# Two transposes of gathered rows ahead of expert weight loads, later counts, and loop registers read behind the last scatter

## The chip, the cores and the metric

The kernel runs on one core of one Trainium2 chip. The metric is the device time of the program in microseconds (us). TensorE (PE) multiplies, VectorE (DVE) and ScalarE (ACT) do elementwise work, GpSimd (POOL) does some of it and issues the indirect DMAs, and SyncE (SP) issues most other DMAs: weight loads, and the DMAs that transpose.

## The reference

Eight batches of eight heads of attention over 576 rows of 64 values, in which only scores within tau of the row's maximum count. Its result, 4608 rows of 512, goes through a mixture of eight experts, one expert to a row:

```python
scores = scale * np.matmul(q, k.transpose(0, 1, 3, 2))
thresh = np.max(scores, axis=-1, keepdims=True) - tau
scores = np.where(scores >= thresh, scores, -1000000000.0)
attn = softmax(scores); out = np.matmul(attn, v)      # x: rows of all heads
expert_idx = np.argmax(x @ w_gate, axis=1)            # gate_w: its softmax value
for e in range(8):
    xe = x[expert_idx == e]
    h = np.maximum(xe @ w1[e], 0.0)                   # 512 -> 1024
    out[expert_idx == e] = gate_w * (h @ w2[e])       # 1024 -> 512
```

## The kernel before, in words

The program has two parts that overlap. The first is the attention of 32 pairs of heads. After each batch its 576 rows of x are routed: gate logits (`lg`), rank of each row within its expert (`rk`), and a scatter of the rows into a DRAM buffer `xs`, sorted by expert (L714, issued by POOL). The second part works through slots of 128 rows of `xs`. For a slot `m`, POOL gathers the rows (L956), SP issues a DMA that transposes them (L962, into `xTm_m`; for slots 3 and 4 it writes into the tail of the tile `R_0`, and the profile calls it `R<-R`), PE multiplies with w1 (`h_m`), ACT and DVE apply the ReLU and split the result in two half-precision parts (`hl_m`), PE multiplies with w2 (`y_m`), ACT scales (`o_m`, L1054) and POOL scatters the rows into the result (L1057).

Weights come in pieces of 128 x 1024 floats. `wf_e_c_w` is chunk `c` of w1 (`w` = 0) or w2 (`w` = 1) of expert `e`; SP loads it (`load_w`, L905) into one of eight buffers. ACT and DVE split it into halves (L918, L919): `wb1_0`, `wb2_0` for even experts, `wb1_1`, `wb2_1` for odd ones. A load into a buffer waits until the piece before it in that buffer has been split.

The first slots are filled before attention has ended: slots 0 to 2 (`NF` = 3) from counts after an early batch, slots 3 and 4 from counts (`pc_1`, function `tables1`) later, and the slots from 5 on once the last batch's counts are there. These last counts (`tables2`) need the ranks of batch 7 and a small matmul `pc_2` on PE. `tables3` (`table_late`) works out the late slots' row lists, the experts whose weights a late slot needs (`esi`) and the bounds `from` and `total` of a loop for rows that no slot holds. That loop (`For_i`, L1339) comes last in the program, and here runs no time. Its two bounds are loaded into a register of each engine at L1337 and L1338.

What sets the order. Up to step `KEND - 16` of the attention each engine's order is written out by hand; after that a scheduler places each instruction on its engine from a timeline of its own, in which the program's order, data dependencies and priorities count. The program's order comes from tables of due times (`plan`, `after(n, f)`: `f` goes n steps on; `phase(7, n)`: step n of the last batch; `w1a`, `w1b`: offsets at which weight pieces go). An engine runs its list in order; an instruction that waits holds all that stands behind it.

Of the kernel before, what the change touches and what calls it, by code (L numbers as in the profile page):

```python
# [44 lines left out]
CAP = NTOK  # L45

TUNE = dict(
    lead=10, cast=1, sl=10, ll=15, sp0=6, sps=0, lv=-9, sv=-2, av=2, tr=4, d=2, lg=5, d5=2, d6=2, d7=1, lg7=9, km=16, rate=15, dh=1, do=3, w1d=5, plv=1, xv=3, so=0, sto=0, ord=0, sc=5, fa=3, fd=4, wa1=-70, wa2=-86, wl1=-28, wl2=-6, avb=2, route=1, ranks=7, pp=8, ew=4, maskat=0, w1a=-40, w1b=3,
)


# [1 line left out]
def kernel(  # L53
# [594 lines left out]
    def route(b, n, dist, Lj, w, got):  # L648
# [38 lines left out]
        def ranks():  # L687
# [32 lines left out]
                sent.add((b, j))  # L720

            if b in TABLES:
                after(phase(7, 10 if b == B - 3 else 18), TABLES[b], FRONT)
            for j in range(n):
                after(6 + dist * j, lambda j=j: send(j))

# [164 lines left out]
    def open_pool(i):  # L891
# [5 lines left out]
        wb1.append(mp.tile([P, 4, 2 * F], F16, name=f"wb1_{i}", bufs=1))  # L897
        wb2.append(mp.tile([P, 4, 2 * F], F16, name=f"wb2_{i}", bufs=1))

    def load_w(e, w, c):  # L900

        i = int(e != 0)
        wq[e, w, c] = wf = pools[i].tile([P, F], F32, tag="wf", name=f"wf_{e}_{c}_{w}", bufs=2 + 6 * i)
        if e in range(E):
            nc.sync.dma_start(wf, w12[e, :, c, w])  # L905
            return
        if e not in regs:
            regs[e] = nc.sync.value_load(T["esi"][0:1, e - E:e - E + 1], min_val=0, max_val=E - 1)
        nc.sync.dma_start(wf, w12[ds(regs[e], 1), :, c, w].rearrange("o p f -> (o p) f"))
# [17 lines left out]
    def fetch(m):  # L927
# [21 lines left out]
        for z in range(1 + (late(m) and tail(m) > 0)):  # L949
            dst = xT[:, i]  # L950
            if late(m):
                Rm = row(B - 1, z if m == "x" else (2 * m + z) % 5)
                w = P + tail(m)
                dst = xT.rearrange("p i c t -> p (i c t)")[:, 0:8 * w].rearrange("p (c t) -> p c t", c=8)
                d["xT"], dst = dst, dst[:, :, P * z:P + tail(m) * z]
            dma = nc.gpsimd.indirect_dma_start(  # L956
                Rm, None, xs[:, :], bass.IndirectOffsetOnAxis(ap=idx[:, z:z + 1].bitcast(U32), axis=0)
            )
            for x in sends:
                tc.add_manual_dep(dma.ins, x.name, SYNC)  # L960
            tc.add_to_no_dep_group("xs", dma.ins)
            nc.sync.dma_start_transpose(dst, Rm[0:tail(m) if z else P, 0:DM].bitcast(F16))  # L962
            gt = small.tile([P, 2], I32, tag="gt", name=f"gt_{m}_{z}", bufs=6)
            gw, ti = gt.bitcast(F32)[:, 0:1], gt[:, 1:2]

            def where(Rm=Rm, gw=gw, ti=ti, z=z):
                nc.vector.tensor_copy(gw, Rm.bitcast(F32)[:, DM:DM + 1])
                to = Rm[:, DM + 1:DM + 2]
                if z:
                    nc.gpsimd.tensor_tensor(ti, to, to, ALU.add)  # L970
                    if tail(m) < P2:
                        nc.gpsimd.tensor_tensor(ti, ti, ti, ALU.add)
                    to = ti
                nc.gpsimd.tensor_tensor(ti, to, bad[:, z:z + 1], ALU.add)

            if m == "x":
                where()
            else:
                after(6, where)
            d["gw"].append(gw)  # L980
            d["ti"].append(ti)
# [11 lines left out]
    def gemm1(g):  # L993
# [14 lines left out]
        for u in range(8 // per):  # L1008
            ph = ps_sc.tile([P, 512], F32, tag="sc", name=f"h_{g[0]}_{u}")
            k = 0  # L1010
            for q in range(per):
                f = slice((per * u + q) * P, (per * u + q + 1) * P)
                o = ph[:, q * w:(q + 1) * w]
                for c in range(4):
                    for z, (wh, xh) in enumerate(((0, 0), (0, 1), (1, 0))):
                        x = xT[:, 2 * c + xh] if late(g[0]) else xT[:, 0:n, 2 * c + xh]
                        tie = g == groups[0] and u == q == c == z == 0
                        emit(o, Wt[:, c, wh, f], x, tie=tie, start=c == 0 and z == 0, stop=c == 3 and z == 2)
                        k += w
                        if k >= 12 * P and (q, c, z) != (per - 1, 3, 2):  # L1020
                            k -= 12 * P
                            yield
            moe(chunk[0] + DH, lambda: True, lambda ph=ph, u=u: relu(ph, u))
            yield

    def gemm2(g):
        d = ms[g]
# [2 lines left out]
        for i in range(len(d["ti"])):  # L1030
# [17 lines left out]
            def leave(i=i, m=m, y=y, half=half, r=r):  # L1048
# [7 lines left out]
                def put():  # L1056
                    dma = nc.gpsimd.indirect_dma_start(  # L1057
                        to, bass.IndirectOffsetOnAxis(ap=d["ti"][i].bitcast(U32), axis=0), o, None,
                        bounds_check=top - 1, oob_is_err=False,
                    )  # L1060
                    if m != "x":
                        tc.declare_no_dep(dma.ins, group="out", reason="each row of the result is written once")
                        tc.add_to_no_dep_group("out", dma.ins)
# [97 lines left out]
    def tables2():  # L1161
# [4 lines left out]
        nc.vector.tensor_scalar(s_e, s_e, float(NE * P), None, ALU.add)  # L1166
        nc.vector.tensor_tensor(s_e, s_e, cnt, ALU.min)
        T[2] = cnt, s_e
        after(20, tables3)

    def tables3():
        T["row"], T["bad"], T["esi"], T["from"], T["total"], static = table_late(*T[2])
# [2 lines left out]

    def experts():

        for i in range(len(groups) + 1):
            if i < len(groups):
                assert there(groups[i], 0)  # L1180
                yield from gemm1(groups[i])
                past[0] = groups[i][-1]
            if i:
                assert there(groups[i - 1], 1)
                yield from gemm2(groups[i - 1])
                past[1] = groups[i - 1][-1]

    def room():
        ldp.close()
# [144 lines left out]
            chunk[0] += 1  # L1334


    total = nc.values_load(T["total"][0:1, 0:1], min_val=0, max_val=NLX)  # L1337
    start = nc.values_load(T["from"][0:1, 0:1], min_val=0, max_val=NL)  # L1338
    with tc.For_i(start, total) as m:  # L1339
        idx = small.tile([P, 2], I32, tag="idx", name="idx_x", bufs=1)  # L1340
        nc.vector.tensor_copy(idx.unsqueeze(1), T["row"][:, ds(m, 1)])
# [67 lines left out]
```

## Time and profile before

| what | value |
|---|---|
| median of 3 runs | 952.98 us (950.48 to 954.14) |
| the profiled execution's own time | 956.04 us |
| its span, first to last instruction | 953.9 us |
| mean granted TensorE clock | 0.986 |
| PE busy | 910.9 us, 95% of the span |
| DVE, ACT, POOL busy | 643.5, 618.3, 560.9 us |
| bytes moved by DMA | 158.14 MB, mean 166 GB/s |

The profiled execution lasts 2.1 us longer than its span and 3.1 us longer than the median of the runs. Busy time of an engine does not count the issuing of DMAs, so SP has none; its work is seen in the rows `SPq`, which are its queue of instructions. "idle before <-releaser" on a row of a timeline says how long the engine stood idle ahead of it and what let it go on. The columns of the table of windows are the stretch, its length, then busy time and count for each engine, then the granted clock, the mean busy share of the DMA engines and the bytes that they moved in GB/s.

### The profile page before, as it was taken

Reading aid. Unit: us, or ns where it says so; the run is one execution under the profiler, and the core shown is the slowest. Engines: PE = TensorE matmul, PEld = TensorE weight load, DVE = VectorE, ACT = ScalarE, POOL = GpSimd, SP = SyncE. Lnnn points to the kernel's source line nnn. Section 1 sums busy time; section 2 is a strip of 40 time slices with the busy share of each in tenths; the row PEclk is TensorE's granted clock in tenths of the full one; section 3 lists DMA queues with packets and bytes.
Section 4 is the critical chain, followed back from the end, with each engine's and each line's share of the span. In section 5 each row is a group of like instructions: output and inputs, shape, how many; then the busy total and the mean of one; then the engine's idle time right before and its main releaser. Section 6 shows DMA issues by size and latency. Waiting matters only on the chain. (4 is left out here: it accounts for less than half of the span.)

```text
span 953.9 us, 25125 instructions
## 1 busy us (share of the span) xinstructions
PE 910.9 (95%) x9983; PEld 641.9 (67%) x9983; DVE 643.5 (67%) x1322; ACT 618.3 (65%) x1042; POOL 560.9 (59%) x482
## 2 busy tenths in 40 slices
PE   4899999999999999999998997999999999999995
PEld 1377777676777777776765966776667766667773
DVE  7989898989898889897986767535143333514561
ACT  4788988888989988888877744335243342524551
POOL 7678787998989989989867625431212121221121
PEclk8899999999999999999999998999999999999998
DMA  7554464585674956756737798986474656547630
GB/s 196 134 139 113 120 150 127 147 184 124 170 162 131 182 128 165 167 134 153 137 95 152 207 283 261 291 228 196 135 243 120 211 156 185 168 142 235 215 121 25
DMA packets 179859, 158.14 MB, mean 166 GB/s; under 512 B 136153, under 2 KB 152027, under 8 KB 179740
## 3 DMA queue, kind: packets, MB, share of 16 engines
q1 hardware_dynamic: 127158, 99.94, 42.1%
q10 hardware_dynamic: 43590, 27.39, 10.9%
q0 software_dynamic: 8992, 29.18, 9.4%
q8 instruction: 80, 1.31, 0.6%
q14 instruction: 39, 0.32, 0.1%
HBM read 90.56 MB, written 19.17 MB: 115 GB/s over the span
## 5 line engine op out<-in xcount | busy, mean ns | idle before, releaser
L489 POOL TENSOR_TENSOR pl<-e,ph 128x1024 f16<-128x1024 f32 x95 | 204.6, 2156 | 52.1 <-ACT ph L488 48.3
L415 DVE TENSOR_REDUCE nm<-s 128x1 f32<-128x512 f32 (+1 forms) x320 | 201.3, 634 | 5.6 <-PE st L388 1.0
L388 PEld LDWEIGHTS <-wb 128*128 128x128 f16 x2304 | 186.4, 99 | 25.9 <-issue 7.7
L388 PE MATMUL y<-wb,hl 128*128 128x512 f16 (+2 forms) x1104 | 196.3, 347 | 0.0
L388 PE MATMUL h<-xTm,wb 128*128 128x256 f16 (+3 forms) x2112 | 191.5, 251 | 2.7 <-issue 2.6
L919 DVE SCALAR_TENSOR_TENSOR wb<-wf,wb 128x1024 f16<-128x1024 f32 x96 | 115.5, 1236 | 58.1 <-ACT wb L918 56.3
L388 PEld LDWEIGHTS <-hl 128*128 128x128 f16 (+2 forms) x1104 | 89.1, 98 | 97.5 <-issue 1.3
L483 DVE SCALAR_TENSOR_TENSOR e<-st,e 128x512 f32<-128x512 f32 x192 | 129.0, 674 | 37.4 <-POOL pl L489 23.2
L403 PE MATMUL s<-QK 128*128 128x512 f16 (+3 forms) x640 | 139.1, 294 | 12.4 <-POOL QK L135 8.1
L480 ACT ACTIVATE e<-st,ntau 128x512 f32<-128x512 f32 x192 | 130.0, 688 | 23.9 <-PE st L388 22.7
L405 PE MATMUL s<-ck,CQ 128*128 128x512 f16 (+3 forms) x640 | 143.5, 292 | 0.5 <-DMA ck<-lo 0.5
L452 PE MATMUL st<-QK 128*128 128x512 f16 (+3 forms) x640 | 137.1, 291 | 5.0 <-DVE e L465 2.6
L388 PE MATMUL st<-CQ,ck 128*128 128x512 f16 (+3 forms) x640 | 132.1, 288 | 0.8 <-DMA CQ<-ptT 0.7
L1057 POOL DMA_INDIRECT out_dram<-o,gt x39 | 41.9, 1074 | 139.0 <-ACT o L1054 128.0
L1005 ACT ACTIVATE hl<-h 128x512 f16<-128x512 f32 (+2 forms) x78 | 44.6, 572 | 115.2 <-PE h L388 96.2
L918 ACT ACTIVATE wb<-wf 128x1024 f16<-128x1024 f32 x96 | 97.6, 1049 | 31.0 <-DMA wf<-in_w_dram 14.0
L531 PE MATMUL av<-vf,e 128*128 128x65 f32 (+1 forms) x1024 | 116.4, 251 | 0.0
L464 ACT ACTIVATE e<-st,ntau_f 128x512 f32<-128x512 f32 (+1 forms) x160 | 94.4, 611 | 26.2 <-PE st L388 23.3
L531 PEld LDWEIGHTS av<-vf,e 128*128 128x128 f32 (+1 forms) x1024 | 101.5, 165 | 0.2
L488 ACT CAST ph<-e 128x1024 f16<-128x1024 f32 x96 | 99.4, 1036 | 1.1 <-DVE e L483 0.9
L535 PE MATMUL av<-vop,pl 128*128 128x65 f16 x768 | 96.5, 193 | 0.0
L534 PE MATMUL av<-vop,ph 128*128 128x64 f16 x768 | 96.2, 193 | 0.0
(225 smaller groups left out, 1482.2 us busy)
## 6 DMA issues: line engine op xcount, KB each, us to landing
wf<-in_w_dram SPq DMA_DIRECT2D x96, 512.0 KB
qkf<-in_qk_dram ACTq DMA_DIRECT2D x29, 576.0 KB
vf<-in_v_dram ACTq DMA_DIRECT2D x30, 320.0 KB
QK<-hi SPq DMA_DIRECT2D x61, 144.0 KB
QK<-hi SPq DMA_DIRECT2D x61, 72.0 KB
QK<-lo SPq DMA_DIRECT2D x61, 72.0 KB
ck<-lo SPq DMA_DIRECT2D x61, 72.0 KB
CQ<-hi SPq DMA_DIRECT2D x61, 64.0 KB
```

Of the source, the lines that this page charges most:

```text
L388: x = nc.tensor.matmul(*a, **kw).ins
L403: nc.tensor.matmul(sc[rows, oc], d["QA"][a][:, cols], d["KB"][a][:, CH[c]], start=True, stop=False)
L405: nc.tensor.matmul(sc[rows, oc], d["CQ"][:, at:at + cols.stop - cols.start], d["CK"][a][:, CH[c]], start=False, stop=True,)
L415: nc.vector.tensor_reduce(o, sc[:, 0:width(t)], axis=AX.X, op=ALU.max, negate=True)
L452: nc.tensor.matmul(sc[rows, oc], d["KB"][a][:, cols], d["QA"][a][:, CH[c]], start=True, stop=False)
L480: nc.scalar.activation(pf, sc, AF.Exp, bias=ntau, scale=0.125 / SS)
L483: nc.vector.scalar_tensor_tensor(pf, sc, 0.0, pf, ALU.is_ge, ALU.mult)
L488: nc.scalar.copy(h, pd)
L489: (nc.vector if (n, t) in PLV else nc.gpsimd).tensor_tensor(l, pd, h, ALU.subtract)
L531: nc.tensor.matmul(av[rows, a], d["Pf"][t][:, q], vf[:, tv], start=False, stop=last)
L918: nc.scalar.activation(o[:, :, 0], x, AF.Copy, scale=SW)
L919: nc.vector.scalar_tensor_tensor(o[:, :, 1], x, SW, o[:, :, 0], ALU.mult, ALU.subtract)
```

## The change

Five things are changed. (1) The two transposes of slots 3 and 4 are remembered (`turned`), and each weight load of experts 1 and 2 that is written after them gets an order edge behind the second of them. The edge is for the scheduler alone; no semaphore comes of it. (2) The pieces of w1 go by `w1a` = -34 where it was -40, and the last batch's tables at step 22 of the batch where it was 18. (3) `tables3` comes 150 steps after the last counts where it was 20. (4) The order of the two multiplications around slot 3 is turned: `gemm2` of slot 2 is written ahead of `gemm1` of slot 3, and the first matmul of slot 3 is tied to that place. (5) POOL copies the loop's two bounds into a tile `ends` behind the last scatter, and the registers of all engines are loaded from `ends`.

```diff
--- before.py
+++ after.py
@@ -45,7 +45,7 @@
 CAP = NTOK
 
 TUNE = dict(
-    lead=10, cast=1, sl=10, ll=15, sp0=6, sps=0, lv=-9, sv=-2, av=2, tr=4, d=2, lg=5, d5=2, d6=2, d7=1, lg7=9, km=16, rate=15, dh=1, do=3, w1d=5, plv=1, xv=3, so=0, sto=0, ord=0, sc=5, fa=3, fd=4, wa1=-70, wa2=-86, wl1=-28, wl2=-6, avb=2, route=1, ranks=7, pp=8, ew=4, maskat=0, w1a=-40, w1b=3,
+    lead=10, cast=1, sl=10, ll=15, sp0=6, sps=0, lv=-9, sv=-2, av=2, tr=4, d=2, lg=5, d5=2, d6=2, d7=1, lg7=9, km=16, rate=15, dh=1, do=3, w1d=5, plv=1, xv=3, so=0, sto=0, ord=0, sc=5, fa=3, fd=4, wa1=-70, wa2=-86, wl1=-28, wl2=-6, avb=2, route=1, ranks=7, pp=8, ew=4, maskat=0, w1a=-34, w1b=3,
 )
 
 
@@ -720,7 +720,7 @@
                 sent.add((b, j))
 
             if b in TABLES:
-                after(phase(7, 10 if b == B - 3 else 18), TABLES[b], FRONT)
+                after(phase(7, 10 if b == B - 3 else 18 if b < B - 1 else 22), TABLES[b], FRONT)
             for j in range(n):
                 after(6 + dist * j, lambda j=j: send(j))
 
@@ -897,12 +897,17 @@
         wb1.append(mp.tile([P, 4, 2 * F], F16, name=f"wb1_{i}", bufs=1))
         wb2.append(mp.tile([P, 4, 2 * F], F16, name=f"wb2_{i}", bufs=1))
 
+    turned = {}
+    BEHIND = mybir.DependencyInfo(mybir.DependencyClass.NoSync, mybir.DependencyReason.SCHED_ONLY)
+
     def load_w(e, w, c):
 
         i = int(e != 0)
         wq[e, w, c] = wf = pools[i].tile([P, F], F32, tag="wf", name=f"wf_{e}_{c}_{w}", bufs=2 + 6 * i)
         if e in range(E):
-            nc.sync.dma_start(wf, w12[e, :, c, w])
+            dma = nc.sync.dma_start(wf, w12[e, :, c, w])
+            if e in (1, 2) and NF + 1 in turned:
+                tc.add_manual_dep(dma.ins, turned[NF + 1].ins.name, BEHIND)
             return
         if e not in regs:
             regs[e] = nc.sync.value_load(T["esi"][0:1, e - E:e - E + 1], min_val=0, max_val=E - 1)
@@ -959,7 +964,7 @@
             for x in sends:
                 tc.add_manual_dep(dma.ins, x.name, SYNC)
             tc.add_to_no_dep_group("xs", dma.ins)
-            nc.sync.dma_start_transpose(dst, Rm[0:tail(m) if z else P, 0:DM].bitcast(F16))
+            turned[m] = nc.sync.dma_start_transpose(dst, Rm[0:tail(m) if z else P, 0:DM].bitcast(F16))
             gt = small.tile([P, 2], I32, tag="gt", name=f"gt_{m}_{z}", bufs=6)
             gw, ti = gt.bitcast(F32)[:, 0:1], gt[:, 1:2]
 
@@ -1014,7 +1019,7 @@
                 for c in range(4):
                     for z, (wh, xh) in enumerate(((0, 0), (0, 1), (1, 0))):
                         x = xT[:, 2 * c + xh] if late(g[0]) else xT[:, 0:n, 2 * c + xh]
-                        tie = g == groups[0] and u == q == c == z == 0
+                        tie = g in (groups[0], groups[NF]) and u == q == c == z == 0
                         emit(o, Wt[:, c, wh, f], x, tie=tie, start=c == 0 and z == 0, stop=c == 3 and z == 2)
                         k += w
                         if k >= 12 * P and (q, c, z) != (per - 1, 3, 2):
@@ -1022,6 +1027,8 @@
                             yield
             moe(chunk[0] + DH, lambda: True, lambda ph=ph, u=u: relu(ph, u))
             yield
+
+    put_last = [None]
 
     def gemm2(g):
         d = ms[g]
@@ -1058,6 +1065,7 @@
                         to, bass.IndirectOffsetOnAxis(ap=d["ti"][i].bitcast(U32), axis=0), o, None,
                         bounds_check=top - 1, oob_is_err=False,
                     )
+                    put_last[0] = dma.ins
                     if m != "x":
                         tc.declare_no_dep(dma.ins, group="out", reason="each row of the result is written once")
                         tc.add_to_no_dep_group("out", dma.ins)
@@ -1166,7 +1174,7 @@
         nc.vector.tensor_scalar(s_e, s_e, float(NE * P), None, ALU.add)
         nc.vector.tensor_tensor(s_e, s_e, cnt, ALU.min)
         T[2] = cnt, s_e
-        after(20, tables3)
+        after(150, tables3)
 
     def tables3():
         T["row"], T["bad"], T["esi"], T["from"], T["total"], static = table_late(*T[2])
@@ -1175,15 +1183,13 @@
 
     def experts():
 
-        for i in range(len(groups) + 1):
-            if i < len(groups):
-                assert there(groups[i], 0)
-                yield from gemm1(groups[i])
-                past[0] = groups[i][-1]
-            if i:
-                assert there(groups[i - 1], 1)
-                yield from gemm2(groups[i - 1])
-                past[1] = groups[i - 1][-1]
+        for i, w in [
+            (i - w, w) for i in range(len(groups) + 1) for w in ((1, 0) if i == NF else (0, 1))
+            if 0 <= i - w < len(groups)
+        ]:
+            assert there(groups[i], w)
+            yield from (gemm1, gemm2)[w](groups[i])
+            past[w] = groups[i][-1]
 
     def room():
         ldp.close()
@@ -1334,8 +1340,11 @@
             chunk[0] += 1
 
 
-    total = nc.values_load(T["total"][0:1, 0:1], min_val=0, max_val=NLX)
-    start = nc.values_load(T["from"][0:1, 0:1], min_val=0, max_val=NL)
+    ends = tp.tile([P, 2], I32, name="ends")
+    for i, x in enumerate(("total", "from")):
+        tc.add_manual_dep(nc.gpsimd.tensor_copy(ends[:, i:i + 1], T[x]).ins, put_last[0].name, BEHIND)
+    total = nc.values_load(ends[0:1, 0:1], min_val=0, max_val=NLX)
+    start = nc.values_load(ends[0:1, 1:2], min_val=0, max_val=NL)
     with tc.For_i(start, total) as m:
         idx = small.tile([P, 2], I32, tag="idx", name="idx_x", bufs=1)
         nc.vector.tensor_copy(idx.unsqueeze(1), T["row"][:, ds(m, 1)])
```

Three places show what moves. The first is on SP and PE around the routing of batch 7. SP before, from the ninth last instruction ahead of the `R_0` transposes (`xTg_7` are the transposes of batch 7's rows for its gate logits, and stand above these rows):

```order
L905 DMA wf_2_1_0_10871<-in_w12_dram 128x1024
L905 DMA wf_1_3_0_10898<-in_w12_dram 128x1024
L905 DMA wf_2_0_1_10942<-in_w12_dram 128x1024
L905 DMA wf_1_0_1_10974<-in_w12_dram 128x1024
L905 DMA wf_2_2_0_10978<-in_w12_dram 128x1024
L905 DMA wf_2_1_1_11003<-in_w12_dram 128x1024
L905 DMA wf_1_1_1_11016<-in_w12_dram 128x1024
L905 DMA wf_2_3_0_11023<-in_w12_dram 128x1024
L905 DMA wf_1_2_1_11073<-in_w12_dram 128x1024
L962 DMA_TRANSPOSE R_0_197<-R_0_197 128x8x128 x2
L905 DMA wf_2_2_1_11078<-in_w12_dram 128x1024
L905 DMA wf_1_3_1_11151<-in_w12_dram 128x1024
```

SP now, from the `xTg_7` transposes on:

```order
L616 DMA_TRANSPOSE xTg_7_0_10690<-R_1_198 128x8x128 x2
L616 DMA_TRANSPOSE xTg_7_2_10720<-R_1_198 128x8x128 x2
L616 DMA_TRANSPOSE xTg_7_4_10732<-Rh_1_200 128x8x128
L967 DMA_TRANSPOSE R_0_197<-R_0_197 128x8x128 x2
L908 DMA wf_1_3_0_10890<-in_w12_dram 128x1024
L908 DMA wf_2_0_0_10934<-in_w12_dram 128x1024
L908 DMA wf_1_0_1_10966<-in_w12_dram 128x1024
L908 DMA wf_2_1_0_10970<-in_w12_dram 128x1024
L908 DMA wf_2_0_1_10995<-in_w12_dram 128x1024
L908 DMA wf_1_1_1_11008<-in_w12_dram 128x1024
L908 DMA wf_2_2_0_11015<-in_w12_dram 128x1024
```

The two transposes stood behind nine weight loads and now stand ahead of them, right behind the gate's; `wf_2_0_0`, which stood ahead of the gate's transposes, follows too. On PE, the last counts stood before the first matmul of slot 3, with the ranks and a last piece of slot 2 ahead:

```order
L696 MATMUL rk_7_10987<-was_7_10893,ones_151 128x40
L388 LDWEIGHTS hl_2_0_10901
L388 MATMUL y_2_0_11159<-wb2_0_9263,hl_2_0_10901 128x512
L388 LDWEIGHTS ones_151
L388 MATMUL pc_2_11179<-run_173,ones_151 128x8
L388 LDWEIGHTS wb1_0_9262
L388 MATMUL h_3_0_11030<-R_0_197,wb1_0_9262 128x128
```

Now slot 2's `y` ends and slot 3 begins with no counts between them:

```order
L388 MATMUL y_2_0_11022<-wb2_0_9263,hl_2_0_10893 128x512
L388 LDWEIGHTS hl_2_0_10893
L388 MATMUL y_2_0_11022<-wb2_0_9263,hl_2_0_10893 128x512
L388 LDWEIGHTS wb1_0_9262
L388 MATMUL h_3_0_11079<-R_0_197,wb1_0_9262 128x128
```

The counts' matmul `pc_2` now stands in the first half of slot 4's `h_4`. Further on PE now runs `y_3`, `y_4`, `h_5`, `h_6`, `y_5`, `h_7`, `y_6`, `h_8`; before it ran `y_3` with the first part of `h_5` inside, the rest of `h_5`, `y_4`, `h_6`, `y_5`, `h_7`, `y_6`, `h_8`. The number of PE's instructions is the same.

The second place is SP around the transposes of the late slots. Before:

```order
L905 DMA wf_2_2_1_11078<-in_w12_dram 128x1024
L905 DMA wf_1_3_1_11151<-in_w12_dram 128x1024
L1337 TENSOR_LOAD total_11460
L1337 ISA x2
L962 DMA_TRANSPOSE xTm_5_11044<-R_1_198 128x8x128
L905 DMA wf_2_3_1_11155<-in_w12_dram 128x1024
L905 DMA wf_3_0_0_11242<-in_w12_dram 128x1024
L962 DMA_TRANSPOSE xTm_6_11163<-R_1_198 128x8x128
L905 DMA wf_3_1_0_11335<-in_w12_dram 128x1024
L962 DMA_TRANSPOSE xTm_7_11329<-R_1_198 128x8x128
L905 DMA wf_3_0_1_11464<-in_w12_dram 128x1024
L905 DMA wf_3_2_0_11468<-in_w12_dram 128x1024
```

Now:

```order
L908 DMA wf_2_2_1_11075<-in_w12_dram 128x1024
L908 DMA wf_2_3_1_11122<-in_w12_dram 128x1024
L908 DMA wf_3_0_0_11245<-in_w12_dram 128x1024
L908 DMA wf_3_1_0_11335<-in_w12_dram 128x1024
L908 DMA wf_3_0_1_11377<-in_w12_dram 128x1024
L908 DMA wf_3_2_0_11381<-in_w12_dram 128x1024
L908 DMA wf_3_1_1_11440<-in_w12_dram 128x1024
L908 DMA wf_3_3_0_11468<-in_w12_dram 128x1024
L967 DMA_TRANSPOSE xTm_5_11027<-R_1_198 128x8x128
L908 DMA wf_3_2_1_11499<-in_w12_dram 128x1024
L908 DMA wf_3_3_1_11558<-in_w12_dram 128x1024
L967 DMA_TRANSPOSE xTm_6_11092<-R_1_198 128x8x128
```

`xTm_5`, which had eleven weight loads between the gate's transposes and itself, now has nineteen, and all but the last two pieces of expert 3 stand ahead of it. The loads of `total` into SP's register are gone from here; the four of `esi` stand behind `xTm_6`.

The third place is the end of POOL's list, behind the scatters of the last slots. Before:

```order
L1057 DMA out_0_dram<-o_34_1_15205,gt_34_1_14264 18432x128
L1057 DMA out_0_dram<-o_35_0_15235,gt_35_0_14485 4608x512
L1337 TENSOR_LOAD total_11460
L1338 TENSOR_LOAD from_11458
L1339 COMPARE_AND_BRANCH
```

Now:

```order
L1064 DMA out_0_dram<-o_34_1_15205,gt_34_1_14264 18432x128
L1064 DMA out_0_dram<-o_35_0_15235,gt_35_0_14485 4608x512
L1345 COPY ends_15240<-total_12440 128x1
L1345 COPY ends_15240<-from_12438 128x1
L1346 TENSOR_LOAD ends_15240
L1347 TENSOR_LOAD ends_15240
L1348 COMPARE_AND_BRANCH
```

The two register loads have two copies ahead of them on POOL. On PE, ACT, DVE and SP, the loads of `total` and `from`, which stood at several places, now read `ends`, and so follow the copies.

## The prediction

> **What bounds the kernel now.** I first read the page's table of the span in 40 slices and its busy times.
>
> ```profile
> span 953.9 us, 25125 instructions
> PE 910.9 (95%) x9983; PEld 641.9 (67%) x9983; DVE 643.5 (67%) x1322; ACT 618.3 (65%) x1042; POOL 560.9 (59%) x482
> PE   4899999999999999999998997999999999999995
> PEclk8899999999999999999999998999999999999998
> ```
>
> PE is busy for 95% of the span, and its instructions stay the same in number and kind. So the time can change only where PE stands idle or runs at a lowered clock. The slices show one such dip inside, at the 25th (572 to 596 us), and the ends. The timeline of PE around the dip tells what it waits for.
>
> ```profile
> 567.04 8.79 PE L388 MATMUL y<-wb,hl 128*128 128x512 f16 x40
> 575.83 0.38 PE L388 MATMUL y<-wb,hl 128*128 128x512 f16 x1
> 579.09 0.19 PE L388 MATMUL pc<-run,ones 128*128 128x8 f16 x1 [2.88 <-DVE posi L706]
> 580.02 6.90 PE L388 MATMUL h<-R,wb 128*128 128x128 f16 x73 [0.74 <-DMA R<-R]
> 606.88 5.34 PE L388 MATMUL y<-wb,hl 128*128 128x512 f16 x24
> 612.06 5.52 PE L388 MATMUL h<-xTm,wb 128*128 128x128 f16 x96
> 635.06 10.64 PE L388 MATMUL h<-xTm,wb 128*128 128x256 f16 x96
> ```
>
> PE first waits 2.88 us for the ranks of batch 7 (through the last counts' matmul, `pc`), and then 0.74 us for slot 3's transpose. An `h` of a 128-row slot costs 5.52 us and a `y` 5.34. At 635.06 the first wide slot, `h_8`, begins; I take it as the point up to which before and after are compared. The windows view, cut at the ends of these stretches, gives the clock and what the DMA engines carried.
>
> ```profile
> 560.00:576.20 16.20, 16.20 (x179) 10.33 (x175) 7.60 (x25) 4.91 (x8) 4.50 (x6) 1.00 1.04 350
> 576.20:580.02 3.82, 0.19 (x2) 0.13 (x2) 3.02 (x14) 1.92 (x5) 1.38 (x2) 0.84 1.13 276
> 580.02:585.64 5.62, 5.62 (x54) 5.62 (x54) 5.31 (x26) 0.18 (x1) 4.40 (x5) 0.50 0.91 290
> 585.64:596.34 10.70, 8.74 (x142) 7.82 (x141) 7.18 (x18) 6.41 (x8) 6.00 (x6) 1.00 0.77 206
> 606.88:635.06 28.18, 26.95 (x267) 17.84 (x265) 8.28 (x32) 8.14 (x11) 8.30 (x10) 1.00 0.95 258
> ```
>
> PE is idle for 3.82 - 0.19 = 3.63 us, and in the 5.62 us that follow the granted clock is 0.50, half of full speed: 2.81 us more. Of the rest, 10.70 - 8.74 = 1.96 and 28.18 - 26.95 = 1.23 us are short stops that the timeline puts down to "issue". Now SP's queue, to see why the transpose was late.
>
> ```profile
> 561.11 12.82 SPq L905 DMA_DIRECT2D wf<-in_w_dram  x9
> 574.11 4.63 SPq L962 DMA_TRANSPOSE R<-R  x2
> 590.73 2.59 SPq L962 DMA_TRANSPOSE xTm<-R  x1
> 564.03 0.99 POOL L956 DMA_INDIRECT R<-xs,row  x1 [2.64 <-DVE row L749]
> 565.33 0.97 POOL L956 DMA_INDIRECT R<-xs,row  x1 [0.30 <-issue]
> ```
>
> The rows of slots 3 and 4 were asked for at 564.03 and 565.33, but their transposes are issued only at 574.11, behind nine loads that take SP from 561.11 on. They leave SP at 578.74 and PE goes on at 580.02, so a transpose lands some 1.28 us behind its issue.
>
> **What the change takes away.** With slot 2's `y` ahead of slot 3's `h` and the counts' matmul inside `h_4`, PE needs no ranks at 576.20. The transposes follow the gathers at the pace that slot 5 shows:
>
> ```profile
> 586.69 0.98 POOL L956 DMA_INDIRECT R<-xs,row  x1 [0.30 <-issue]
> L962 SPq DMA_TRANSPOSE xTm<-R x27: 1212/1252/10397, 590.7 to 888.1; - x27
> ```
>
> From gather to transpose went 590.73 - 586.69 = 4.04 us, and a transpose that waits for nothing takes SP 1.25 us. So they start at 564.03 + 4.04 = 568.07 and 565.33 + 4.04 = 569.37 and leave SP at about 570.7, landed by 572.0, before PE wants them. Idle time and low clock go: 3.63 + 2.81 = 6.44 us.
>
> **What it adds in the queue.** From 561.11 until 570.7, SP now stands at the transposes and carries no weights. Then come nineteen loads, and only behind them `xTm_5`. PE reaches `h_5` after two `h`, two `y` and, if the 1.96 us of issue stops stay, at 576.20 + 2 x 5.52 + 2 x 5.34 + 1.96 = 599.88. When has `xTm_5` landed? Three rates come from the trace. The rows of ACT's timeline where a split waited for its load give one:
>
> ```profile
> 567.69 1.06 ACT L918 ACTIVATE wb<-wf 128x1024 f16<-128x1024 f32 x1 [2.36 <-DMA wf<-in_w_dram]
> 575.42 1.06 ACT L918 ACTIVATE wb<-wf 128x1024 f16<-128x1024 f32 x1 [2.40 <-DMA wf<-in_w_dram]
> wf<-in_w_dram SPq DMA_DIRECT2D x96, 512.0 KB
> ```
>
> These two are the second and the seventh load of the nine: 7.73 / 5 = 1.55 us a load, with two gathers moving beside them.
>
> - Issue alone: 12.82 / 9 = 1.42 us a load. 570.7 + 19 x 1.42 = 597.7, and the transpose's 1.25 on SP and 1.28 to land make 600.2.
> - Loads at the pace of arrival, 1.55: 570.7 + 29.4 + 2.5 = 602.6.
> - By bytes: 19 x 0.524 MB = 9.96, and POOL's transfers on the same DMA engines in that time. These are a scatter of the result for each of slots 1 to 3, the five scatters of batch 7's rows, which start near 580, and the gathers of slots 5 and 6: ten at 128 x 514 x 4 bytes = 0.263 MB. In all 12.59 MB. The window 560 to 576.20 moved 350 GB/s with a DMA share of 1.04, that is, with the DMA engines full: 36.0 us, 606.7, landed at 609.2. At the 290 GB/s of 580.02 to 585.64, when the scatters ran, it is 43.4 us and 616.6.
>
> I take 609.2: the scatters are small-row traffic that the first two rates leave out, and the window of 350 GB/s is the nearest with loads, gathers and scatters of the result together. The window's share of 1.04 at 350 GB/s is the row to hold against a rule of the Trainium skill (Perfetto Trace Analysis, section Roofline), that one core alone may pull more than its 358 GB/s share up to about 435 of its DMA engines. By it the estimate is 12.59 / 0.435 = 28.9 us and 602.1, so it speaks for the second rival below; the trace has the engines full at 350.
>
> The splits do not slow the loads: ACT takes 1.06 us for one and shares them with DVE, less than 1.42. The last counts now come with `pc_2` in `h_4`, some 4 us later than at 579.09, so slot 5's gather moves from 586.69 to about 591 and its rows are there at 595: earlier than SP comes to `xTm_5`, at 606.7. Hence it is SP's queue that decides, and 4 us of the counts are covered; with the cover gone they would be 0 at a PE that arrives at 599.88.
>
> **The sum.** From the moment `xTm_5` lands, PE has three `h`, two `y`, the 1.23 us of issue stops and, after an idle time of 609.2 - 599.88 = 9.3 us, again a stretch at half clock like the 2.81 before: 27.24 + 1.23 + 2.81 = 31.28 us. `h_8` begins at 609.2 + 31.28 = 640.5, against 635.06: +5.4 us. After 640 PE's row of the 40 slices stands at 9 up to the last, so nothing there wins the 5.4 back. `xTm_6` stands two loads behind `xTm_5`, 2 x 1.55 + 1.25 = 4.4 us, less than `h_5` (5.52), hidden. `xTm_7` comes behind the `esi` loads; `tables3`'s 150 steps could make these late, which I price at 0 to 2 us in the range.
>
> **The end.** The chain of what ended last, and the branch of the loop:
>
> ```profile
> 945.11 0.02 POOLq L1057
> 945.13 3.11 issue
> 948.24 0.51 POOLq L1337
> 948.74 0.69 POOL out_dram L1057
> L1339 PEldq COMPARE_BRANCH  x3: 104/185/3546, 941.5 to 952.4; - x3
> L1057 POOL DMA_INDIRECT out_dram<-o,gt x39: 967/1012/1947, 560.4 to 948.4; - x39
> 574.50 0.35 POOL L974 TENSOR_TENSOR gt<-R,badi 128x1 int32<-128x1 int32 x2
> ```
>
> The last scatter was issued 3.11 us later than its data allowed, for a reason that no row shows. Now the registers come from copies behind that scatter. PE's branch of 3.55 us, which ran 944.49 to 948.04 beside the scatter, now starts after the scatter (1.0 us), two copies (0.2 each, an estimate from POOL's row of two small integer operations, 0.35) and two register loads (0.51 each). Without the 3.11 us the scatter starts at about 945.4, that branch at 947.8 and it ends at 951.4; with them it is 950.9 and 954.4. The span ended at 953.9, so the end lies 0 us off or some 3 us later. I take 0, since the register load next to the hole is gone from there; the other end is a rival. The row of 3546 ns beside 104 and 185 fits what the Trainium skill says (Runtime: NRT & Kernel Launch, section Instruction fetch mechanics), that a taken branch to code not yet fetched stalls; by it the later branch costs its 3.55 us in full after the registers, the +3 case.
>
> The profiled execution took 956.04 us, 3.1 more than the median of the runs, and the sum is made on its rows. Nothing in it hangs on that offset, so I put it on the median: 952.98 + 5.4 = 958.4 us.
>
> **The rivals.** A measurement of this kernel can tell about 0.5% from no change, 948.2 to 957.7.
>
> 1. Forecast, the stall moves from slot 3 to slot 5: `xTm_5` lands between 606 and 617, h_8 at +2 to +13; 955 to 966. Chance 0.48, of which 0.07 is inside the bound.
> 2. The loads drain at 1.55 us each: landing at 602.6, a stall of 2.7 in place of 3.63. 602.6 + 28.47 - 635.06 = -4.0 without a low clock, -1.2 with one: 949 to 952. For it speaks the pace of arrival, against it the scatters between. Chance 0.23, nearly all "same".
> 3. Faster, at the point where `xTm_5` lands before 600: SP issues at 1.42 us a load throughout, the stall and the low clock are simply gone, 6.4 us, 946.5. For it speaks that the weights of expert 3 are no hurry to anyone and the DMA share was 0.77 at 585 to 596, room that the move could use. Against it: 19 loads in 27 us are 369 GB/s for the weights alone, more than any window above shows for all transfers. Chance 0.19.
> 4. The end: the hole of 3.11 us stays, and the branch follows the copies: +3 on top of the second case, or of the first. 954 to 961. Chance 0.06.
> 5. The change does not do what it says: the gathers of slots 3 and 4 land only after 574, SP holds its queue that much longer, and PE waits at 576 as before, with `xTm_5` later too: near 960. Nothing in the trace shows when these gathers land; the 4.04 us of slot 5 speak against it. Chance 0.04.
>
> Slower: 0.41 of the first, most of the fourth and the fifth, 0.49. Same: 0.29. Faster: 0.22. The likeliest case's own range is 955 to 966. The range for 8 in 10 must hold the third case as well: 945.5 to 966.
>
> **What would show it.** In PE's timeline after: no gap before the first `h<-R`, and a gap of 6 to 17 us before the first `h<-xTm` of slot 5, with the transpose as its releaser, near 609, and a clock below 1.00 behind it. In SP's: `R<-R` issued by 571, then some nineteen loads, then the transpose after 605. If the gap is under 3 us, the second or third case holds. If SP's `R<-R` ends after 574, the first step is wrong. At the end, `PEldq COMPARE_BRANCH` starts after the last scatter; whether the chain of waits still has its 3.11 us of issue ahead of that scatter decides between 0 and +3.

## The result

The changed kernel takes 962.81 us (median of 4 runs, 962.17 to 966.03) where the kernel before takes 952.53 us in the same comparison: ratio 1.0116, 95% interval 1.0086 to 1.0146, so 10 us slower. The forecast was 958.4, slower, with a range of 945.5 to 966.

The profiled execution of the changed kernel took 962.17 us. Its page and its timeline of PE, from the first matmul of slot 3 to the first wide slot:

```profile
span 960.1 us, 25130 instructions
...
573.30 6.19 PE L388 MATMUL h<-R,wb 128*128 128x128 f16 x108
579.33 0.17 PE L388 MATMUL pc<-run,ones 128*128 128x8 f16 x1
594.01 0.38 PE L388 MATMUL y<-wb,hl 128*128 128x512 f16 x1 [0.42 <-ACT wb L923]
596.25 2.29 PE L388 MATMUL y<-wb,hl 128*128 128x512 f16 x5 [1.86 <-DVE wb L924]
604.75 7.83 PE L388 MATMUL h<-xTm,wb 128*128 128x128 f16 x96 [6.21 <-DMA xTm<-R]
615.27 7.16 PE L388 MATMUL h<-xTm,wb 128*128 128x128 f16 x96 [2.68 <-DMA xTm<-R]
637.99 10.64 PE L388 MATMUL h<-xTm,wb 128*128 128x256 f16 x96
```

Slot 3 begins without a wait, and the last counts sit inside `h_4` at no cost. But PE waits 0.42 + 1.86 = 2.28 us for the halves of expert 1's last w2 piece, 6.21 us for slot 5's transpose and 2.68 us for slot 6's. The two `h` behind these waits take 7.83 and 7.16 us where 5.52 is the rule, 3.95 us more. The windows view has the lowered clock there (columns: stretch, length, busy of PE, PEld, DVE, ACT, POOL, granted clock, DMA share, GB/s):

```profile
573.30:604.75 31.45, 22.91 (x242) 15.49 (x241) 24.80 (x66) 15.77 (x21) 15.16 (x15) 0.86 1.05 375
604.75:615.27 10.52, 7.83 (x96) 7.66 (x96) 5.48 (x36) 1.19 (x2) 1.79 (x4) 0.77 1.14 244
615.27:622.27 7.00, 7.00 (x97) 7.00 (x97) 1.39 (x3) 0.60 (x1) 4.16 (x6) 0.76 0.82 203
```

SP's queue after:

```profile
564.99 2.61 SPq L967 DMA_TRANSPOSE R<-R  x2
567.69 28.86 SPq L908 DMA_DIRECT2D wf<-in_w_dram  x19
596.66 3.66 SPq L967 DMA_TRANSPOSE xTm<-R  x1
600.42 1.01 SPq L908 DMA_DIRECT2D wf<-in_w_dram  x2
601.52 13.38 SPq L967 DMA_TRANSPOSE xTm<-R  x3
```

The transposes of slots 3 and 4 go out 9 us sooner than before, and nineteen loads at 28.86 / 19 = 1.52 us each follow. Slot 5's transpose is issued at 596.66, and PE goes on at 604.75: 8.1 us later, not 2.5. SP's issue runs ahead of the data, so at 596.66 the loads in front are still moving: from 596.66 to 600.32, when SP issues no load, its DMA queue carries 1.39 MB, as much as 2.7 loads. Slot 6's is issued at 601.52 and used at 615.27.

The end of the program, with ACT's last scaling, POOL's last scatter and copy, and PE's branch:

```profile
946.74 0.69 ACT L1061 ACTIVATE o<-y,gt 128x512 f32<-128x512 f32 x1 [4.60 <-PE y L388]
950.80 0.98 POOL L1064 DMA_INDIRECT out_dram<-o,gt  x1 [6.91 <-issue]
951.90 0.19 POOL L1345 COPY ends<-from 128x1 int32<-128x1 int32 x1
L1348 PEldq COMPARE_BRANCH  x3: 100/200/3902, 953.4 to 959.0; - x3
```

The scatter still starts 3.4 us behind the scaling's end, and PE's branch of 3.90 us now runs behind copies and register loads, alone: it starts at 953.7, and 2.5 us more follow it up to the end of the span.

To compare runs I cut each profile at three points: PE's first gate matmul of the last batch (`lg`), the first matmul of the second wide slot (`h_10`; PE's work between the two is the same in every kernel, but that without the edge 14 matmuls of `y_2` more stand ahead of the first cut, some 3 us), and ACT's last scaling. I call the three pieces behind `lg` the stage, the middle and the end. Before: 566.04, 650.72, 944.39, span 953.9, so stage 84.68, middle 293.7, end 9.5. After: 563.25, 653.65, 946.74, 960.1, so 90.40, 293.1 and 13.4. The change costs 5.7 us in the stage and 3.8 in the end, 9.5 together, with 0.6 less in the middle; the 2.8 us by which the changed kernel's `lg` came earlier lie in the attention part, so the spans are 6.2 us apart. The profiled execution of before was itself 3.5 us over its median, which is why the medians are further apart. In its stage are 3.1 us of short stops of PE, which the changed kernel does not have; they are taken up below.

### The profile page after: what moved, and what is told of

Same layout as the page of the kernel before. It is cut to its first block, busy times and chain, and to the rows that moved or that the text cites. A ratio compares the mean times of both kernels' runs of the same rounds, so it can differ in the third digit from the quotient of the medians.

```text
span 960.1 us, 25130 instructions
## 1 busy us (share of the span) xinstructions
PE 907.2 (94%) x9983; PEld 641.9 (67%) x9983; DVE 649.1 (68%) x1322; ACT 617.7 (64%) x1042; POOL 558.0 (58%) x484
## 4 chain that ended last, share of the span: by engine, by line
PE 70%; DMA 8%; POOL 7%; DVE 7%; issue 4%; SPq 3%; ACT 2%; ACTq 0%; POOLq 0%
PE h L388 19%; PE y L388 18%; PE av L531 5%; PE st L452 5%; PE s L403 5%; PE s L405 5%; PE st L388 5%; POOL pl L489 3%; DMA wf<-in_w_dram 3%; PE av L525 3%; DVE nm L415 2%; PE av L535 2%; PE av L536 2%; PE av L534 2%; DMA xTm<-R 1%
## 5 line engine op out<-in xcount | busy, mean ns | idle before, releaser
L388 PE MATMUL h<-xTm,wb 128*128 128x256 f16 (+3 forms) x2112 | 193.7, 254 | 8.9 <-DMA xTm<-R 8.9
L924 DVE SCALAR_TENSOR_TENSOR wb<-wf,wb 128x1024 f16<-128x1024 f32 x96 | 118.8, 1270 | 64.3 <-ACT wb L923 62.8
L465 DVE SCALAR_TENSOR_TENSOR e<-st,e 128x512 f32<-128x512 f32 (+1 forms) x160 | 90.9, 585 | 7.9 <-ACT e L464 7.1
```

The costliest lines, as they stand in the source:

```text
L388: x = nc.tensor.matmul(*a, **kw).ins
L924: nc.vector.scalar_tensor_tensor(o[:, :, 1], x, SW, o[:, :, 0], ALU.mult, ALU.subtract)
```

## The experiments

The theory: the order edge, which sends the transposes of slots 3 and 4 ahead, makes slot 5 and slot 6 late by their place in SP's queue; the new end costs by itself. Rivals: the DMA engines are full, so the place does not matter; the later counts and tables make slot 5 late; the end is free. In all of them `end` means the piece above. Ratios are to the kernel before in the same comparison, and a cost in us behind a ratio is worked out from the ratio; the medians can differ from it by about 1 us.

**The end alone, and all but the end.** The first kernel is before with only this edit, the second is the changed one without it:

```diff
-    total = nc.values_load(T["total"][0:1, 0:1], min_val=0, max_val=NLX)
-    start = nc.values_load(T["from"][0:1, 0:1], min_val=0, max_val=NL)
+    ends = tp.tile([P, 2], I32, name="ends")
+    for i, x in enumerate(("total", "from")):
+        tc.add_manual_dep(nc.gpsimd.tensor_copy(ends[:, i:i + 1], T[x]).ins, put_last[0].name, BEHIND)
+    total = nc.values_load(ends[0:1, 0:1], min_val=0, max_val=NLX)
+    start = nc.values_load(ends[0:1, 1:2], min_val=0, max_val=NL)
```

> The kernel before with only the end of the change: the loop's bounds copied by POOL behind the last scatter, the registers of all engines loaded from there; all weights, tables and matmuls in the old order. Theory (the end costs by itself, since PE's 3.9 us branch follows the copies): about +3.8 us, 956.4. Rival (the end is free, the whole +10.3 us comes from SP's queue): within 1 us of before, 952.5.

> The changed kernel with the end of before (registers loaded from total and from, wherever the order puts them). Theory: 962.8 - 3.8 = 959.0, with PE still waiting some 6 us for slot 5's transpose. Rival (the end is free): 962.8.

The end alone: 955.98 us, ratio 1.0038 (1.0018 to 1.0059), so +3.6 us. All but the end: 961.37, 1.0087 (1.0054 to 1.0121), so +8.3. The theory's 3.8 holds for the first; for the second the end's share comes out at 11.0 - 8.3 = 2.7, with 11.0 for the ratio 1.0116, less than 3.8 but inside the two intervals. In the profile of the first the branch stands behind the copies as in the changed kernel:

```profile
941.49 0.69 ACT L1061 ACTIVATE o<-y,gt 128x512 f32<-128x512 f32 x1 [4.61 <-PE y L388]
945.54 0.98 POOL L1064 DMA_INDIRECT out_dram<-o,gt  x1 [6.92 <-issue]
L1348 PEldq COMPARE_BRANCH  x3: 100/193/3625, 948.3 to 953.6; - x3
```

Its end is 954.7 - 941.49 = 13.2 us. The end of all but the end is 959.1 - 949.48 = 9.6. Over all profiles of this study, kernels with the loop have an end of 9.4 to 9.7 us with the old registers (eight) and of 12.8 to 13.4 with the new ones (five). Here the rival falls: the end is not free. That PE's branch stalls is also what the Trainium skill has (Runtime: NRT & Kernel Launch, section Instruction fetch mechanics: a taken branch to code outside the fetched pages stalls); the trace fits it, with 3.3 to 3.9 us in each kernel that has the loop, where the other engines' branches take 0.03 to 0.06, but no row shows what PE waits for in it. With the old registers this branch is hidden beside the last scatter.

**Slots 5 and 6 ahead of expert 3's loads.** The edit to the changed kernel, one edge more:

```diff
             if e in (1, 2) and NF + 1 in turned:
                 tc.add_manual_dep(dma.ins, turned[NF + 1].ins.name, BEHIND)
+            for m in (5,):
+                if e == 3 and m in turned:
+                    tc.add_manual_dep(dma.ins, turned[m].ins.name, BEHIND)
```

> The changed kernel, and the eight weight loads of expert 3 get an order edge behind slot 5's transpose; on SP the transposes of slots 5 and 6 then stand behind thirteen loads in place of nineteen and twenty-one, nothing else is moved there. Theory (place in SP's queue decides): the waits of 6.2 and 2.7 us for slots 5 and 6 go, and with them the low clock (3.95 us): 962.8 - 12.8 = 950, up to 953 if the gathers themselves are late (slot 5's rows landed about 594 in the changed kernel). Rival (the DMA engines are full with bytes, the place does not matter): 962.8, with the wait for slot 5 where it was.

948.47 us, ratio 0.9960 (0.9939 to 0.9981), where the changed kernel has 1.0116. SP's queue and PE in it:

```profile
565.76 18.01 SPq L908 DMA_DIRECT2D wf<-in_w_dram  x13
592.14 2.72 SPq L970 DMA_TRANSPOSE xTm<-R  x2
594.96 4.65 SPq L908 DMA_DIRECT2D wf<-in_w_dram  x8
```

```profile
594.73 1.24 PE L388 MATMUL y<-wb,hl 128*128 128x512 f16 x5 [1.86 <-DVE wb L927]
595.80 10.88 PE L388 MATMUL h<-xTm,wb 128*128 128x128 f16 x192
606.52 10.52 PE L388 MATMUL y<-wb,hl 128*128 128x512 f16 x48
637.90 10.64 PE L388 MATMUL h<-xTm,wb 128*128 128x256 f16 x96
```

Slots 5 and 6 follow each other without a wait and at full clock. The stage takes 637.90 - 561.17 = 76.7 us, 13.7 less than in the changed kernel; the expected 12.8 and the time agree. The same loads move the same bytes, so the rival with the full DMA engines falls: it was the place in the queue. SP even stands still ahead of the two transposes, from 583.77 to 592.14, until slot 5's rows are there, and the eight loads that this delays cost PE no wait.

**The same with the end of before.** The edge of the last run added, here with slot 6 in the condition too (`for m in (5, 6)`), and the edit of the end undone. On SP the same thirteen loads stand ahead of the two transposes and the same eight behind:

> As the run with slots 5 and 6 ahead of expert 3's loads, and the end of before. Theory: both costs gone, 950 - 3.8 = 946.2, so 6 us below before: the gain that the change was to have. Rival (bytes): 959.

945.65 us, ratio 0.9927 (0.9902 to 0.9952). It beats both kernels, by 7 us against before, and it is 2.8 us below the kernel with the new end. Repeated on its own on another chip:

> The kernel of the run with slots 5 and 6 ahead and the end of before, once more and on its own. The runs of one stage with the same order of instructions (this one, the one with the fills on POOL, the one without the loop) took 75 to 90 us from the last gate logits to the second wide slot, and PE's short stops of issue, 0 and 7.8 us, came with the slow one. Theory A (leaving out the loop made these stops, by where the code lies): 945 and none of them here, the ratio to before 0.993 as it was. Theory B (they come and go with the chip or its memory, whatever the kernel): 950 to 957 and stops here as well, or a wide spread of the times.

944.61 us, 0.9931 (0.9906 to 0.9955). PE's waits in the stage then are one row:

```profile
PE y L388 <- DVE wb L927: 1.9, 1, 1.9
```

**The edge alone, and all without the edge.** The first is before with `turned` and the edge only; in the second the condition of the edge is off and all else stays, the new end too.

```diff
-            if e in (1, 2) and NF + 1 in turned:
+            if False:
```

> The kernel before with only the order edge (weight loads of experts 1 and 2 behind the transposes of slots 3 and 4); offsets, table times, order of the multiplications and end as before. On SP slot 5's transpose then stands behind twenty weight loads, and slot 5's first multiplication behind slot 4's second one, as in the changed kernel. Theory (the edge alone makes the new stall): PE waits 6 to 8 us for slot 5's transpose and some for slot 6, about +6 us, 958. Rival (the other parts, later counts and later tables, make it): 946 to 952.

> The changed kernel without the order edge, all else as changed, the end too. On SP the transposes of slots 3 and 4 stand behind ten loads again, slot 5's behind thirteen. Theory: PE waits again about 3.7 us for slot 3 with some low clock, hardly for slot 5; with the end's 3.9 us that makes about 956. Rival (later counts and tables make slot 5 late by themselves): the wait for slot 5 stays, 962.

The edge alone: 958.07 us, 1.0052 (1.0025 to 1.0078), +5.0 us with the old end. All without the edge: 957.29, 1.0043 (1.0021 to 1.0066), +4.1 us, of which the end's 3.6 are nearly all. The profiles of the two, SP and PE of the first, then of the second:

```profile
570.28 28.67 SPq L908 DMA_DIRECT2D wf<-in_w_dram  x19
599.07 5.49 SPq L967 DMA_TRANSPOSE xTm<-R  x1
599.79 2.29 PE L388 MATMUL y<-wb,hl 128*128 128x512 f16 x5 [2.30 <-DVE wb L924]
609.68 12.54 PE L388 MATMUL h<-xTm,wb 128*128 128x128 f16 x192 [7.60 <-DMA xTm<-R]
```

```profile
565.02 13.54 SPq L908 DMA_DIRECT2D wf<-in_w_dram  x10
578.75 4.87 SPq L967 DMA_TRANSPOSE R<-R  x2
584.90 8.98 PE L388 MATMUL h<-R,wb 128*128 128x128 f16 x108 [5.99 <-DMA R<-R]
603.67 0.55 PE L388 MATMUL h<-xTm,wb 128*128 128x128 f16 x7 [1.61 <-DMA xTm<-R]
```

With the edge, PE waits 7.6 us for slot 5; without it, 6.0 for slot 3 and 1.6 for slot 5. So the edge alone is enough to move the stall. The edge alone also gave the scheduler a new order on PE (slot 3's `h` ahead of the counts, slot 5's behind `y_4`), which the other edits of the change write out by hand. Later tables and counts are not needed for the stall, as the first run shows; in the second they leave 1.6 us of it, but there PE itself comes to slot 5 late, after its wait at slot 3. The edge alone and the end alone add up to 8.6 us, the whole change to 10 or 11. The intervals allow the difference; what the profiles have for it is the wait for slot 6, 2.7 us in the changed kernel and 3.6 in all but the end, which is not there with the edge alone. Which of the other edits brings that wait was not tested.

**How many loads may stand ahead.** The edge on expert 3's w2 pieces only (`w == 1` in the condition above), in the changed kernel:

> The changed kernel, its end too, with an order edge for only the w2 pieces of expert 3 behind slot 5's transpose: on SP it then stands behind fifteen loads, slot 6's still behind all twenty-one; PE has slot 5's second multiplication ahead of slot 6's first. Theory (each late slot's place in SP's queue decides for that slot): no wait for slot 5, or under 2 us, and a wait of some 6 us for slot 6, whose transpose lands near 613 to 615 as in the changed kernel; 955 to 957. Rival (fifteen loads are as bad as nineteen): 962. Rival (slot 5 alone counted): 950.

962.26 us, 1.0081 (1.0063 to 1.0100). A miss: the time is that of the first rival, and the profile shows neither theory nor rival. PE waits for no transpose at all in it. What it has, on this chip, is many short stops, one row of the waits view (engine, what it waited for, us in total, times, longest):

```profile
PE h L388 <- issue: 7.0, 14, 1.2
```

The windows view has a lowered clock between them, from 583 to 594 us:

```profile
583.00:594.00 11.00, 8.50 (x90) 6.87 (x88) 8.90 (x14) 7.46 (x9) 5.61 (x5) 0.72 1.02 386
```

So the waits went and the time did not. The stage is 87.4 us, 3.0 less than in the changed kernel, with 7.0 us of stops in it; `lg` came 3.0 us later, at 566.27. That slot 6 is not waited for proves little, since the stops make PE come later. How much is the order and how much these stops, this run cannot tell; they are taken up below.

**What the 3.1 us ahead of the last scatter are.** 24 fills of a small tile on POOL behind slot 20's scatter, in the kernel with slots 5 and 6 ahead and the old end; and that kernel without the loop. In these two, and in the two runs after them, the condition names slot 5 alone, as in the first kernel with that edge; in these two SP has the same thirteen loads, two transposes and eight loads.

```diff
                     put_last[0] = dma.ins
+                    if m == 20 and i == 0:
+                        pad = tp.tile([P, 1], F32, name="pad")
+                        for _ in range(24):
+                            x = nc.gpsimd.memset(pad, 0.0)
+                            tc.add_manual_dep(x.ins, dma.ins.name, BEHIND)
```

> The run with slots 5 and 6 ahead and the end of before, and 24 fills of one element per partition on POOL behind slot 20's scatter, which nothing waits for. It asks what the 3.1 us ahead of the last scatter are. Theory A (POOL fetches its next block of code there, the position in its list counts): the hole moves to an earlier scatter, where POOL waits anyway, and the end is 3.1 us sooner, 942.5. Theory B (the hole belongs to the last scatter, whatever stands before it): 945.6 and the 3.1 us stay.

> The run with slots 5 and 6 ahead and the end of before, without the loop at the end and its registers (it leaves out the rows that no slot holds, of which this input has none). Theory A (the 3.1 us before the last scatter and PE's 3.5 us branch both belong to the loop's code): both go, the last scatter starts 0.3 us behind its data, and the time is some 3 us less, 942.5. Theory B (the hole belongs to the last scatter itself): the 3.1 us stay, 945.5.

The fills: 945.00 us, 0.9928, as without them, and the chain that ended last still has the hole:

```profile
932.05 0.02 POOLq L1067
932.07 3.11 issue
935.18 0.51 POOLq L1351
```

Without the loop the last scatter starts as late as ever:

```profile
948.98 0.69 ACT L1064 ACTIVATE o<-y,gt 128x512 f32<-128x512 f32 x1 [3.85 <-PE y L388]
953.03 0.98 POOL L1067 DMA_INDIRECT out_dram<-o,gt  x1 [6.16 <-issue]
```

From the start of ACT's last scaling to the scatter it is 4.05 us here, and 4.05 or 4.06 in every other profile of this study; the chain puts 3.1 us of it to "issue" with the old end and 3.3 with the new one. So the hole belongs to neither the loop, nor the register loads, nor the scatter's place in POOL's list by 24 instructions. What it is stays open. The end without the loop is 956.9 - 948.98 = 7.9 us, 1.6 less than with it. The kernel as a whole took 957.38, 1.0016 (0.9991 to 1.0041), not 942 to 946: its stage took 89.9 us, with stops of issue again:

```profile
PE h L388 <- issue: 7.8, 15, 1.1
```

**Expert 1's pieces first.** In the kernel with slots 5 and 6 ahead and the old end, `w1a=-20, w1b=1`, so that expert 1's last w2 piece is the eighth load and not the eleventh:

> The run with slots 5 and 6 ahead and the end of before, with the pieces of expert 1 asked for closer together (offset -20 and one step apart), so that its last piece of w2 is the eighth load behind the transposes of slots 3 and 4 and not the eleventh. Theory (the 1.9 to 2.3 us that PE waits within y_4 are that piece's place in the queue): the wait goes, 943.5. Rival (slot 5's transpose is late next, since its own gather lands near 594): PE waits the same time one step on, 945.6.

951.71 us, 0.9999 (0.9978 to 1.0019): 6 us worse than without it. The wait within `y_4` went, as the theory had it, and others came, more than the rival had. The scheduler also gave another order: on SP two loads stand between the transposes of slots 5 and 6, and on PE `y_5` begins ahead of `h_6`.

```profile
598.66 5.52 PE L388 MATMUL h<-xTm,wb 128*128 128x128 f16 x96 [1.32 <-DMA xTm<-R]
610.03 0.61 PE L388 MATMUL y<-wb,hl 128*128 128x512 f16 x1 [5.42 <-DVE hl L1014]
```

PE stands 1.3 us for slot 5's transpose and 5.4 for the ReLU and split of slot 5's result on DVE.

**Counts and tables at their old times.** Step 18 and 20 steps in that same kernel:

> The run with slots 5 and 6 ahead and the end of before, with the last batch's tables at step 18 and the late tables after 20 steps, as before. Theory (later counts and late tables have no part in the result once slots 5 and 6 stand ahead; only slot 7 moves on SP): 945.6, no change from that run. Rival (the later tables are what keeps VectorE free for the splits around slots 3 to 5): slower by 2 us or more, with a new wait on DVE in PE's timeline.

954.04 us, 0.9986 (0.9963 to 1.0009), on the chip of the two runs with many stops; it has 3.1 us of them, and no new wait on DVE above 0.3 us. Against 0.9927 it is slower, but with the stops in it this does not show whether the tables' times matter.

**The short stops.** All of them lie in `h` of 128-row slots, none in `y`. Profiles with none: the changed kernel and all eight runs on two chips, and the repeated run on a third. Profiles with some: before (3.1 us), and all three on the fourth chip (7.0, 7.8, 3.1), where the kernel before took 954.76 us and not 950.6 to 952.5. The profile of the end alone has before's order on PE up to the end, and none. So the same order can have them or not, and leaving out the loop is no cause for them, since the other two on that chip have the loop. The same four profiles have a middle of 293.7 us, the ten others one of 293.1, which speaks for something that lasts for a whole execution; on which chip before was profiled is not on record. What starts the stops isn't shown.

## Why the prediction came out as it did

- **The gain.** "6.44 us go": right. No run with the edge has a wait at slot 3, and the counts are covered in all of them but for 0.9 us in the one with expert 1's pieces first.
- **The new stall.** Right in place and kind: slot 5's transpose behind nineteen loads, released by its landing. It landed 604.75 - 573.30 = 31.5 us behind slot 3's start; predicted were 609.2 - 576.20 = 33.0. That the two agree is luck in part. Issue went at 1.52 us a load, near the second rate and not that of the bytes, so the transpose was issued 23.4 us behind slot 3's start and not 30.5; then it took 8.1 us to PE and not 2.5. The 2.5 rested on a misreading of the rows of before: of the two `R<-R` transposes slot 3 needs the first alone, which was on SP for 1.32 us from 574.11 (the second one's last completion in the trace is at 580.9, behind PE's start), so 4.6 us and not 1.28 stood between its leaving SP and PE's start at 580.02, and 5.9 from its issue on.
- **The terms of the stage's sum.** Predicted +5.4, and +5.7 in the profiles between the cuts, yet by terms that make up for each other, and against a profile of before with stops in it: the run with the end alone, which has the order of before and no stops, has a stage of 82.6 us, 7.8 less than the changed kernel's. Not foreseen: 2.28 us for the halves of expert 1's w2 within `y_4`, and 2.68 for slot 6, of which I said "hidden" because two loads and a transpose are 4.4 us of SP; landing, not SP, set it. The low clock cost 5.0 and not 2.81: 3.95 in the two `h`, and 1.05 in the last five matmuls of `y_4`, which took 2.29 us at a granted clock of 0.50 where the run with slots 5 and 6 ahead has 1.24 at 1.00. On the other side, PE's wait for slot 5 was 6.2 and not 9.3 us, and the 3.2 us of short stops that I carried over were none.
- **The step that failed: the end.** "I take 0, since the register load next to the hole is gone from there." The hole stayed at its length with that load gone, and PE's branch came behind the copies. Measured: +3.8 us between the cuts, +3.6 by the run with the end alone. It was in the prediction as the fourth rival, +3, at a chance of 0.06. The only reason given for 0 was that a register load stood next to the hole, and no row ties the two together. The rest of the 3.8 is that the branch started 2.9 us behind the scatter's start and not 2.4, and took 3.90 us and not 3.55. With +3.8 in the sum it gives 962.2, against 962.8.
- **The rivals.** Second and third, the loads drain in time: they do issue at the second's pace, but landing lags issue. Fifth: the gathers were in time, the transposes were off SP at 567.6.
- **The rule on bandwidth** (the Trainium skill, Perfetto Trace Analysis, section Roofline: about 435 GB/s for a lone core). The most that 10 us carry in any profile here is 416 GB/s, at a DMA share of 1.03, in the run with expert 1's pieces first from 575 to 585 us; the changed kernel has 410 from 591 to 601. So the figure was not reached, but nearly. The prediction took 350 GB/s for full engines; that was the mean of a window whose part from 564 to 575 us has 406 at a share of 1.02. A share of about 1 goes with very different rates: in the changed kernel it is 1.22 from 600.32 to 604.75 us, with a transpose, gathers and scatters, at 275 GB/s.

## What to carry to other kernels

An order edge that brings one transfer forward on a queue pushes all that stands behind it; look at what is now last in front of the next consumer, and give that one its edge as well. The changed kernel lost 10 us, and one more edge with the old end turned it into 7 us gained. Price a queue by when its transfers land and not by when the last is issued. Leave loop registers where their branch runs beside other work; a late load puts the whole branch on the end.

## What was not expected of the hardware

- The last scatter starts 4.05 us behind the start of the scaling that feeds it in every kernel here, 3.1 to 3.3 us of it with no releaser, with 24 instructions more ahead of it, with copies behind it and without the loop. The scatters that waited for their scaling start 0.3 to 0.8 us behind its end; the last one starts 3.4 us behind.
- A transpose is on SP for 1.2 to 3.7 us, but PE, waiting for it, went on 5.9 us after its issue (slot 3 before), 8.1 and 13.7 us (slots 5 and 6 in the changed kernel), and 3.1 us (slot 5 in the run with expert 1's pieces first).
- A wait of 1.86 us within `y_4` was followed by a granted clock of 0.50 in the changed kernel and of 1.00 in the run with slots 5 and 6 ahead.
- On one of the four chips on record all three profiles had 3 to 8 us of stops of PE in which it waited for nothing that the trace shows, and the two with the longer ones had stretches at a granted clock of 0.72 to 0.86.
